# HGRN2 attention and an ELU layer on one core: exponentials of every second group one step ahead, second products with the sums last, decays and loads at other steps

## The chip, the core and the metric

The kernel runs on one core of a Trainium2 chip. The time is that of one execution on the device, in microseconds (us); the figure that counts is the median of several executions. A profile is one execution of its own, recorded by the hardware, and its time is compared with itself only. Engines by their names in the profile: PE multiplies matrices (PEld loads its weights), DVE, ACT and POOL work element by element, SP issues transfers (DMA).

## The reference

Two blocks follow each other. The first is a linear attention with a decaying state, for 4 batches of 8 heads, 768 tokens and 48 numbers per head:

```
f = sigmoid(f_logit)
for t in tokens:
    state = f[t] * state + outer(k[t], v[t])
    y[t]  = q[t] @ state
```

The second takes y as 3072 tokens of 384 numbers and computes `elu(x @ w_in) @ w_out` with 2048 hidden numbers, where elu(h) is h above zero and exp(h) - 1 below. Inputs and result are float32 in meaning; the weights arrive as float64 and are cut to float32 in the first part of the kernel.

## The kernel before

**Units.** The 3072 tokens are cut in 12 units of 256. Every unit goes through attention (PE: `transposed`, `advance`, `scores`, `outputs`, `carried`), gives a tile `xt` of sixteen 128x128 blocks, and this tile goes through the layer. The layer of units 0 and 1 is done plainly, in half steps T = 0 to 31 (`up` and `down`). Units 2 to 11 are done by a scheme with fewer products: `blend` (L937) first makes 12 sums of pairs of xt's blocks in six instructions, numbered 0 to 5 here after their place in `X_SUMS`; number 4 writes blocks 8 and 15. Then a unit has four **groups**. A group (`n`, 40 in all) is 256 of the hidden numbers, 20 products of 128x128x128 in five **phases** (`PHASES`, L428; `phase`, L953), written to two PSUM banks. The first product of a unit's first phase reads block 8.

**From a phase to the second product.** ACT copies parts of a bank to a tile `vals` (L967), DVE adds copies and banks to each other (`joins`, L945: `JOIN3` and `MID` after phase 3, `JOIN4` and `LAST` after phase 4). `LAST` completes the hidden numbers h. `exp_quad` (L1269) then gives ACT two pairs of Relu and Exp for the group (L975, L976), and one step later `elu` (L992) lets DVE take the maximum (L995) and POOL make four sums for each of the two halves of the group (L1005), eight POOL instructions. `down` (L1009) multiplies with `w_out` in seven products of 128x128x192 per half, `todo` (L1041). Three of the seven use the elu's result as it is, four use the sums `s`, which POOL makes in the order s[0], s[2], s[1], s[3]. A unit's last half is followed by an evacuation: ACT copies a bank (L1065) and DVE adds up (L1064).

**The order of the work.** All is written out by hand, and each engine runs its instructions in the order of the program. From T = 32 on the loop at L1278 counts **steps** s = 0 to 99, two half steps each (T = 32 + 2s). A step issues, in this order: the plan of the even half step; two phases, with joins; `MID` and `LAST`; the elu's due (L1293); the plan of the odd half step; a fixed number of second products (`CHUNKS`, L1267: 7, 7, 7, 7, 0, 6, 6, 6, 5, 5); the exponentials due (L1298). Ten steps make a unit, with four groups in them. A group with an even number has its `LAST` in the first phase of step 2 or 7 of the ten, one with an odd number in the second phase of step 4 or 9.

**The plan** (`at_step`) places everything else. For a unit u whose base step is t: `load` (L465, eight DMAs on SP), `gates` (L662, two ACT instructions), three `decays` and one `settle` (`D3`, `D4`), `transposed`, `both`, `outputs` and `carried` (`A3`), and `blend` (`BL`). One `decays(p)` (L695) is a scan (L681) and a reciprocal (L686) on DVE, two scalings on POOL (L676; one for p = 0), and for p = 2 two DMAs on SP (`move`, L688). `settle` (L710) is a small DVE instruction and three scalings on POOL. Before the scheme starts, `w_sums` (L576) combines blocks of `w_in` and `combine` (L918) parts of `w_out`, on DVE and POOL.

Of the kernel before, what the change touches and what calls it, by code (L numbers as in the profile page):

```python
# [356 lines left out]
def fast(ctx: ExitStack, tc: tile.TileContext, q, k, v, f_logit, w_in, w_out, out, flag, outer):  # L357
# [18 lines left out]
    nc = tc.nc  # L376
# [29 lines left out]
    A1 = (2, 8, 10, 11)  # L406
    D2 = (16, 18, 20, 22)
    A2 = (23, 25, 25, 26, 27, 28)
    D3 = (-7, -5, -3, -1)
    D4 = (-9, -6, -4, -1)  # L410
    A3 = (3, 9, 12, 13)
    BL = 16
    BL2 = 29
# [13 lines left out]
    EARLY = 10  # L427
# [11 lines left out]
    MID = (ALU.add, (1, 5), (1, 5), None, (9, 11)), (ALU.subtract, (8, 9), (5, 5), None, (8, 12))  # L439
    JOIN4 = (ALU.add, (3, 6), (2, 11), 0, (0, 2)), (ALU.subtract, 2, 3, 0, 3)  # L440
    LAST = ((ALU.add, (3, 7), (3, 10), None, (4, 7)),)
    PLACES = ((6, ((1, 0), (0, 0), (1, 1), (0, 1))), (0, ((0, 1), (1, 1), (1, 0), (0, 0))))
    USUAL = ((0, 0), (0, 1), (1, 0), (1, 1))

    FULL = (slice(0, 64), slice(64, 128))
# [123 lines left out]
    def w_block(q, n):  # L569
        if n >= 12:  # L570
            return extra[:, q, n - 12]
        i, k = divmod(n, NKT)
        i = (0, 2, 3, 1)[i]
        return wis[:, q, i // 2, k, i % 2]

    def w_sums(e, q, some):  # L576
        for to, a, b, sign in W_SUMS[some]:
            e.tensor_tensor(
                out=w_block(q, to), in0=w_block(q, a), in1=w_block(q, b), op=ALU.add if sign > 0 else ALU.subtract
            )  # L580
# [81 lines left out]
    def gates(u, pieces=(NKT,), bias=1):  # L662

        p = 0
        for n in pieces:
            a = qkf[u % NB]["f"][:, p : p + n, 0]
            nc.scalar.activation(a, a, AF.Exp, scale=-1.0)
            if bias:
                nc.scalar.activation(a, a, AF.Copy, bias=1.0)
            p += n  # L670
# [216 lines left out]
    def at_step(step, *todo):  # L887
        plan.setdefault(step, []).extend(todo)
# [48 lines left out]
    def blend(u, e, some):  # L937

        x = xts[u]
        for to, a, b in X_SUMS[some]:  # L940
            e.tensor_tensor(out=pick(x, to), in0=pick(x, a), in1=pick(x, b), op=ALU.subtract)  # L941
# [67 lines left out]
    def down(P):  # L1009
        m, j = order[P]  # L1010
        if j == 0:
            pms[m] = [ps.tile([128, DM], FP32, tag=f"m{i + (m < DIRECT)}", name=f"psM{m}_{i}") for i in range(NW if m < DIRECT else 4)]
        pm, (g, where) = pms[m], gs.pop(P)
        ends = dict(start=(j == 0), stop=(j == NP - 1))
        if m < DIRECT:
            for i in range(2):
                for t in range(NW):
                    nc.tensor.matmul(  # L1018
                        pm[t][:], lhsT=g[:, 2 * i + t], rhs=wo[:, 2 * j + i, :],
                        start=(j == 0 and i == 0), stop=(j == NP - 1 and i == 1),  # L1020
                    )
            if j == NP - 1:
                o = (outer if (NU - m) % 2 else sb).tile([128, 2, DM], FP32, tag="o", name=f"o{m}", bufs=1)
                for t in range(NW):
                    nc.scalar.copy(o[:, t], pm[t][:])
                    t0 = m * U + t * 128
                    nc.sync.dma_start(out=out[t0 : t0 + 128, :], in_=o[:, t])
                del pms[m]
            return
        a = [[g[:, where.index((i, t))] for i in range(2)] for t in range(2)]  # L1030
        b = [[wo[:, 2 * j + i, h * DH : (h + 1) * DH] for h in range(2)] for i in range(2)]
        plain = PLAIN if m == DIRECT else 0
        if j < plain:

            alone = ((3, 0), (2, 0)), ((2, 1), (3, 1))
            todo = [(*alone[t][h], a[t][i], b[i][h]) for i in range(2) for t in range(2) for h in range(2)]
            starts = ((3, 0), (2, 0)) if j == 0 else ()
        else:
            s = ss.pop(P)
            c = [combos[i][:, j] for i in range(4)]  # L1040
            todo = [  # L1041
                (0, 0, a[0][0], b[0][0]), (3, 0, a[0][1], b[1][0]), (0, 1, s[:, 1], c[1]),
                (1, 0, s[:, 0], c[0]), (1, 1, s[:, 2], c[2]), (2, 1, a[1][1], c[3]), (2, 0, s[:, 3], b[1][1]),
            ]
            if j == plain:
                todo = todo[3:] + todo[:3]
            starts = ((0, 0), (3, 0), (1, 0), (2, 1)) if j == 0 else ((0, 0), (1, 0)) if j == plain else ()
        started = set()
        for n, (bank, half, x, y) in enumerate(todo):
            first = (bank, half) in starts and bank not in started  # L1050
            started.add(bank)
            if n:
                yield
            nc.tensor.matmul(  # L1054
                pm[bank][:, half * DH : (half + 1) * DH], lhsT=x, rhs=y,
                start=first, stop=(j == NP - 1), skip_group_check=True,
            )
        if j == NP - 1:
            p = [[pm[i][:, h * DH : (h + 1) * DH] for h in range(2)] for i in range(4)]
            o = (outer if (NU - m) % 2 else sb).tile([128, 2, DM], FP32, tag="o", name=f"o{m}", bufs=1)  # L1060
            u2 = sb.tile([128, DH], FP32, tag="u2", name=f"u2_{m}", bufs=1)
            u43 = sb.tile([128, 2, DH], FP32, tag="u43", name=f"u43_{m}", bufs=1)
            flat = o[:].rearrange("p t f -> p (t f)")
            add = lambda to, x, y: nc.vector.tensor_tensor(out=to, in0=x, in1=y, op=ALU.add)  # L1064
            (nc.vector.tensor_copy if m == NU - 1 else nc.scalar.copy)(u2[:], p[0][0])  # L1065
            add(flat[:, 0:DH], p[3][0], u2[:])
            add(u2[:], p[0][1], u2[:])
            add(u43[:], pm[1][:].rearrange("p (h f) -> p h f", h=2), u2[:].unsqueeze(1).broadcast_to([128, 2, DH]))
            add(flat[:, 3 * DH :], p[1][0], u43[:, 1])
            if plain:  # L1070
                add(flat[:, 3 * DH :], p[3][1], flat[:, 3 * DH :])
            add(flat[:, DH : 3 * DH], pm[2][:], u43[:].rearrange("p h f -> p (h f)"))
            def store(*queues):
                for t in range(2):
                    for h in ((1, 0) if t else (0, 1)):
                        queues[t].dma_start(
                            out=out[m * U + t * 128 : m * U + (t + 1) * 128, h * DH : (h + 1) * DH],
                            in_=o[:, t, h * DH : (h + 1) * DH],
                        )

            if m == NU - 1:
                left.append(store)
            else:
                store(nc.sync, nc.sync)
            del pms[m]
# [70 lines left out]
    a = qkf[1]["f"][:, 0:NKT, 0]  # L1156
# [38 lines left out]
    for n in range(1, NFT):  # L1195
        t = min(max(needs[n][0] - 2, 0), n) + 2 * (n == NFT - 1)
# [17 lines left out]
        at_step(12 + n, lambda n=n: w_sums(nc.gpsimd, slice(0, 2), slice(n, n + 1)))  # L1214
        at_step(22 + n, lambda n=n: w_sums(nc.gpsimd, slice(2, 4), slice(n, n + 1)))
    for n in range(EARLY, len(W_SUMS)):
        at_step(26 + (n - EARLY) // 2, lambda n=n: w_sums(nc.vector, slice(0, 2), slice(n, n + 1)))
        at_step(32 + n - EARLY, lambda n=n: w_sums(nc.gpsimd, slice(2, 4), slice(n, n + 1)))
    at_step(BL2, lambda: blend(2, nc.vector, slice(0, 3)), lambda: blend(2, nc.gpsimd, slice(3, 6)))
    base = lambda u: u * NFT if u < PLAIN_UP else PLAIN_UP * NFT + (u - PLAIN_UP) * 20  # L1220
    for u in range(3, NU):
        t = base(u - 1)
        for n in range(6):
            at_step(t + BL + n // 2, lambda u=u, n=n: blend(u, nc.gpsimd, slice(n, n + 1)))
        at_step(base(u - 2), lambda u=u: load(u))
        at_step(t - (8 if u == 3 else 10), lambda u=u: gates(u))
        attention(u, [t + i for i in (D3 if u == 3 else D4)], [t + i for i in A3])
    for n in range(NR):
        t = base(3) + (base(NU - 1) - base(3)) * n // NR + RR
        at_step(t, lambda n=n: reread(n))  # L1230
# [30 lines left out]
    exps, elus = {}, {}  # L1261

    def take(n):
        for _ in range(n):
            next(stream, None)
# [3 lines left out]
    def exp_quad(n, s):  # L1269
        for i in range(2):  # L1270
            frm, where = PLACES[i]
            P = PLAIN_UP * NP + 2 * n + i
# [5 lines left out]
    for s in range(5 * total // 2):  # L1278
        T = PLAIN_UP * NFT + 2 * s
        for f in plan.pop(T, ()):  # L1280
            f()
        done = []
        for i in (2 * s, 2 * s + 1):
            n, i = divmod(i, 5)
            phase(n, i)
            if i > 2:
                joins(n, JOIN3 if i == 3 else JOIN4)
                done.append((n, MID if i == 3 else LAST))
        for n, todo in done:
            joins(n, todo)  # L1290
            if todo is LAST:
                exps[s + 1] = n
        for P in elus.pop(s, ()):  # L1293
            elu(P)
        for f in plan.pop(T + 1, ()):
            f()
        take((4, 4, 3, 3)[s] if s < 4 else CHUNKS[s % 10])
        if s in exps:  # L1298
            exp_quad(exps.pop(s), s)
# [55 lines left out]
```

## Time and profile before

| what | value |
|---|---|
| median of 3 runs | 587.03 us (585.92 to 589.24) |
| the profiled execution's own time | 588.51 us |
| its span, first to last instruction | 586.7 us |
| busy: PE, DVE, ACT, POOL | 547.3, 391.9, 315.9, 316.8 us |
| granted PE clock, mean | 0.992 |
| one unit in the scheme (second products of step 35 to those of step 45) | 280.27 to 325.24 us |

The time splits into a start with plain units (to about 120 us), nine units with attention beside them, of 45 us each, a last unit without attention, and a tail of second products. In the answers of the trace a line has the start and the length in us, engine, line of the code, operation, output and input tiles, shapes, and in brackets the idle time of the engine before it and what ended that. PE shows two instructions for each float32 product.

### The profile page before, as it was taken

To read this page: it belongs to the slowest core of one execution; us is meant where nothing else is said; L and a number is where in the kernel's file an instruction comes from. 1 tells how busy PE (TensorE), PEld (TensorE's weight loads), DVE (VectorE), ACT (ScalarE), POOL (GpSimd) and SP (SyncE) were. 2 spreads that over 40 slices of the span, in tenths; PEclk is the share of its full clock that TensorE was granted. 3 is DMA by queue.
4 is the path that set the end of the run, shared out by engine and by line. 5 is a ranking of instruction groups with operands and counts; after the bars stand their busy time and mean duration, and the time that the engine had idled before them with its cause. 6 is when DMAs were issued, how large, how long until landed. Compare 5 with 4: busy or idle time off the path is not lost.

```text
span 586.7 us, 15572 instructions
## 1 busy us (share of the span) xinstructions
PE 547.3 (93%) x6294; PEld 495.4 (84%) x6294; DVE 391.9 (67%) x720; ACT 315.9 (54%) x643; POOL 316.8 (54%) x556
## 2 busy tenths in 40 slices
PE   6799999988999999999999999999999999999876
PEld 3477678877989989889889889889889889899775
DVE  8888884977855945845955955864873973643641
ACT  3387853325455664665656656556656646544440
POOL 6600366695673672682682583484484385264343
PEclk9999999989999999999999999999999999999998
DMA  8999880050061081071071161152152121110001
GB/s 206 259 245 232 235 198 10 8 129 29 8 183 56 8 208 54 11 208 34 32 199 37 38 169 52 53 142 75 54 130 88 51 75 29 56 35 1 28 2 32
DMA packets 39473, 54.28 MB, mean 93 GB/s; under 512 B 4032, under 2 KB 29216, under 8 KB 39392
## 3 DMA queue, kind: packets, MB, share of 16 engines
q1 hardware_dynamic: 38592, 52.61, 34.2%
q8 instruction: 51, 0.84, 0.6%
q10 hardware_dynamic: 800, 0.59, 0.5%
q14 instruction: 30, 0.25, 0.1%
HBM read 45.02 MB, written 4.72 MB: 85 GB/s over the span
## 4 chain that ended last, share of the span: by engine, by line
PE 57%; DVE 27%; POOL 5%; issue 5%; ACT 3%; DMA 2%; ACTq 0%; DVEq 0%; POOLq 0%
PE psM L1054 25%; PE psH L961 19%; DVE vals L951 13%; PE psH L985 5%; DVE gg L995 4%; POOL sums L1005 4%; DVE f L686 3%; PE psM L1018 2%; PE psY L802 2%; DVE o L1064 2%; ACT area L630 1%; DVE u L1064 1%; DVE f L681 1%; PE psT L724 1%; DMA f<-f 1%
## 5 line engine op out<-in xcount | busy, mean ns | idle before, releaser
L1005 POOL TENSOR_TENSOR sums<-gg 128x128 f32<-128x128 f32 x172 | 93.0, 560 | 189.3 <-DVE gg L995 178.4
L967 ACT COPY vals<-psH 128x512 f32<-128x512 f32 (+1 forms) x120 | 64.1, 550 | 169.9 <-PE psH L961 100.5
L961 PE MATMUL psH<-xt,wi 128*128 128x128 f32 x880 | 139.1, 277 | 4.2 <-DVE gg L995 2.3
L961 PE MATMUL psH<-xt,area 128*128 128x128 f32 x720 | 126.0, 279 | 2.5 <-DVE vals L951 1.4
L951 DVE TENSOR_TENSOR vals<-vals,psH 128x256 f32<-128x256 f32 (+1 forms) x160 | 61.4, 384 | 98.0 <-PE psH L961 51.3
L961 PEld LDWEIGHTS psH<-xt,wi 128*128 128x128 f32 x880 | 118.7, 193 | 7.0 <-issue 3.5
L1054 PE MATMUL psM<-area,sums 128*128 128x192 f32 x516 | 107.8, 338 | 15.6 <-POOL sums L1005 15.6
L961 PEld LDWEIGHTS psH<-xt,area 128*128 128x128 f32 x720 | 104.2, 192 | 6.6 <-POOL xt L941 3.7
L1054 PEld LDWEIGHTS psM<-area,sums 128*128 128x128 f32 x516 | 84.1, 191 | 23.9 <-POOL sums L1005 21.9
L1054 PE MATMUL psM<-wo,gg 128*128 128x192 f32 x376 | 77.2, 330 | 1.9 <-DVE gg L995 1.6
L1054 PEld LDWEIGHTS psM<-wo,gg 128*128 128x128 f32 x376 | 62.1, 192 | 4.0 <-DVE gg L995 3.8
L686 DVE RECIPROCAL f<-f 128x256 f32<-128x256 f32 x36 | 62.8, 1748 | 1.1
L976 ACT ACTIVATE gg<-gg 128x512 f32<-128x512 f32 x96 | 60.5, 630 | 3.1
L951 DVE TENSOR_TENSOR vals<-vals 128x256 f32<-128x256 f32 x120 | 56.4, 483 | 2.1
L676 POOL TENSOR_TENSOR k<-k,f 128x256 f32<-128x256 f32 x48 | 39.0, 815 | 29.2 <-DVE f L681 19.0
L995 DVE SCALAR_TENSOR_TENSOR gg<-gg,vals 128x512 f32<-128x512 f32 x80 | 51.6, 685 | 0.8 <-ACT gg L976 0.5
L975 ACT ACTIVATE gg<-vals 128x512 f32<-128x512 f32 x80 | 49.6, 620 | 3.2 <-DVE vals L951 3.2
L985 PE MATMUL psH<-xt,wi 128*128 128x256 f32 x192 | 45.1, 384 | 2.3 <-DVE xt L883 1.7
L676 POOL TENSOR_TENSOR q<-q,f 128x256 f32<-128x256 f32 x48 | 37.0, 771 | 18.8 <-DMA f<-f 15.7
L1064 DVE TENSOR_TENSOR o<-psM,u 128x192 f32<-128x192 f32 (+1 forms) x33 | 13.1, 421 | 50.4 <-ACT u L1065 50.0
L1005 POOL TENSOR_TENSOR sums<-gg,sums 128x128 f32<-128x128 f32 x86 | 43.0, 500 | 6.7
L1054 PE MATMUL psM<-wo,sums 128*128 128x192 f32 x172 | 43.4, 334 | 0.4
(110 smaller groups left out, 771.2 us busy)
## 6 DMA issues: line engine op xcount, KB each, us to landing
area<-in_moe_w_out_dram SPq DMA_DIRECT2D x8, 768.0 KB, 10.8
again<-in_moe_w_in_dram SPq DMA_DIRECT2D x16, 384.0 KB, 4.9
again<-in_moe_w_out_dram SPq DMA_DIRECT2D x16, 384.0 KB, 3.8
k<-in_k_dram SPq DMA_DIRECT2D x12, 384.0 KB, 4.4
q<-in_q_dram SPq DMA_DIRECT2D x12, 384.0 KB, 5.5
v<-in_v_dram SPq DMA_DIRECT2D x12, 384.0 KB, 5.9
area<-in_moe_w_in_dram SPq DMA_DIRECT2D x8, 576.0 KB, 9.2
out_dram<-o SPq DMA_DIRECT2D x42, 96.0 KB, 1.7
```

The costliest lines, as they stand in the source:

```text
L676: e.tensor_tensor(out=t[n][:, p], in0=t[n][:, p], in1=t["f"][:, p, "kq".index(n)], op=ALU.mult)
L686: nc.vector.reciprocal(f[:, p, 1], f[:, p, 0])
L951: nc.vector.tensor_tensor(out=pick(v, to), in0=x, in1=y, op=op)
L961: nc.tensor.matmul(bank[:, slot], lhsT=w_block(q, w), rhs=xts[m][:, x], start=(i < 2 and t == 0), stop=True, skip_group_check=True,)
L967: nc.scalar.copy(v[:, at : at + size], bank[:, frm : frm + size])
L975: nc.scalar.activation(g[:], h, AF.Relu, scale=-1.0)
L976: nc.scalar.activation(g[:], g[:], AF.Exp, scale=-1.0)
L985: nc.tensor.matmul(ph[:, i], lhsT=wi[j][:, kt, i * 128 : (i + 1) * 128], rhs=xts[m][:, 2 * kt : 2 * kt + 2].rearrange("n t f -> n (t f)"), ...
L995: nc.vector.scalar_tensor_tensor(out=g[:], in0=g[:], scalar=-1.0, in1=phs.pop(P), op0=ALU.add, op1=ALU.max)
L1005: nc.gpsimd.tensor_tensor(out=s[:, i], in0=x, in1=y, op=op)
L1054: nc.tensor.matmul(pm[bank][:, half * DH : (half + 1) * DH], lhsT=x, rhs=y, start=first, stop=(j == NP - 1), skip_group_check=True,)
L1064: add = lambda to, x, y: nc.vector.tensor_tensor(out=to, in0=x, in1=y, op=ALU.add)
```

## The change

- `D3` of (-7, -5, -3, -1) becomes (-9, -6, -3, 1); `D4` of (-9, -6, -4, -1) becomes (-17, -15, -5, 1) and is for unit 4 alone; later units have `D5` = (-19, -15, -5, 1). The numbers are half steps, counted from t.
- Exponentials of groups with an even number are issued at the end of the step of their `LAST`, not of the next; their elu's follow one step earlier too.
- In `exp_quad` the two halves of a group change places, and `w_block` changes the blocks of `w_in` accordingly.
- In `down` the product (2, 1), which needs no sum, moves from the sixth place to the third; the product (0, 1), which needs s[1], from the third to the sixth.
- `blend`: two of six instructions in each of the half steps 16, 17, 18 become four in 16 and two in 18.
- `load` and `gates` move: load by 0 half steps for unit 3, 3 for unit 4, 6 for the others ahead; gates from 8 or 10 half steps ahead of t to 11, 19 and 21.
- Nine `w_sums` on DVE start at T = 23, not 26.

No instruction is added or left out.

```diff
-    D3 = (-7, -5, -3, -1)
-    D4 = (-9, -6, -4, -1)
+    D3 = (-9, -6, -3, 1)
+    D4 = (-17, -15, -5, 1)
+    D5 = (-19, -15, -5, 1)
...
-    PLACES = ((6, ((1, 0), (0, 0), (1, 1), (0, 1))), (0, ((0, 1), (1, 1), (1, 0), (0, 0))))
+    PLACES = ((0, ((0, 1), (1, 1), (1, 0), (0, 0))), (6, ((1, 0), (0, 0), (1, 1), (0, 1))))
...
-        i = (0, 2, 3, 1)[i]
+        i = (2, 0, 1, 3)[i]
...
-                (0, 0, a[0][0], b[0][0]), (3, 0, a[0][1], b[1][0]), (0, 1, s[:, 1], c[1]),
-                (1, 0, s[:, 0], c[0]), (1, 1, s[:, 2], c[2]), (2, 1, a[1][1], c[3]), (2, 0, s[:, 3], b[1][1]),
+                (0, 0, a[0][0], b[0][0]), (3, 0, a[0][1], b[1][0]), (2, 1, a[1][1], c[3]),
+                (1, 0, s[:, 0], c[0]), (1, 1, s[:, 2], c[2]), (0, 1, s[:, 1], c[1]), (2, 0, s[:, 3], b[1][1]),
             ]
             if j == plain:
-                todo = todo[3:] + todo[:3]
+                todo = todo[2:5] + todo[:2] + todo[5:]
...
-        at_step(26 + (n - EARLY) // 2, lambda n=n: w_sums(nc.vector, slice(0, 2), slice(n, n + 1)))
+        at_step(23 + (n - EARLY) // 2, lambda n=n: w_sums(nc.vector, slice(0, 2), slice(n, n + 1)))
...
-            at_step(t + BL + n // 2, lambda u=u, n=n: blend(u, nc.gpsimd, slice(n, n + 1)))
-        at_step(base(u - 2), lambda u=u: load(u))
-        at_step(t - (8 if u == 3 else 10), lambda u=u: gates(u))
-        attention(u, [t + i for i in (D3 if u == 3 else D4)], [t + i for i in A3])
+            at_step(t + BL + n // 4 * 2, lambda u=u, n=n: blend(u, nc.gpsimd, slice(n, n + 1)))
+        at_step(base(u - 2) - (0, 3, 6)[min(u - 3, 2)], lambda u=u: load(u))
+        at_step(t - (11, 19, 21)[min(u - 3, 2)], lambda u=u: gates(u))
+        attention(u, [t + i for i in (D3, D4, D5)[min(u - 3, 2)]], [t + i for i in A3])
...
             if todo is LAST:
-                exps[s + 1] = n
+                exps[s + n % 2] = n
```

## The prediction

> **What bounds the kernel now.** I read the busy times first, then PE's waits, then the timelines of one unit.
>
> ```profile
> span 586.7 us, 15572 instructions
> PE 547.3 (93%) x6294; PEld 495.4 (84%) x6294; DVE 391.9 (67%) x720; ACT 315.9 (54%) x643; POOL 316.8 (54%) x556
> ...
> PE psM L1054 <- POOL sums L1005: 15.6, 21, 1.4
> ```
>
> PE is busy for 93% of the span, so only its waits can go, 39 us in all, a part of them at the start. The largest is that second products wait for POOL's sums, 21 times. PE through one unit, step 35 to 45:
>
> ```profile
> 280.27 1.01 PE L1054 MATMUL psM<-area,sums 128*128 128x192 f32 x4 [0.51 <-POOL sums L1005]
> ...
> 282.81 1.16 PE L802 MATMUL psY<-at,v 64*64 64x64 f32 x64
> ...
> 292.88 0.68 PE L961 MATMUL psH<-xt,wi 128*128 128x128 f32 x4 [0.18 <-DVE vals L951]
> ...
> 296.81 0.38 PE L961 MATMUL psH<-xt,area 128*128 128x128 f32 x2
> ...
> 299.67 0.49 PE L1054 MATMUL psM<-wo,sums 128*128 128x192 f32 x2
> 300.25 0.94 PE L961 MATMUL psH<-xt,area 128*128 128x128 f32 x6
> ...
> 302.34 0.92 PE L1054 MATMUL psM<-wo,gg 128*128 128x192 f32 x4
> 304.08 1.24 PE L1054 MATMUL psM<-area,sums 128*128 128x192 f32 x6 [0.82 <-POOL sums L1005]
> ...
> 305.81 0.38 PE L961 MATMUL psH<-xt,area 128*128 128x128 f32 x2
> ...
> 308.47 0.82 PE L1054 MATMUL psM<-wo,gg 128*128 128x192 f32 x4
> ...
> 310.75 0.38 PE L961 MATMUL psH<-xt,area 128*128 128x128 f32 x2
> ...
> 322.84 0.94 PE L961 MATMUL psH<-xt,area 128*128 128x128 f32 x6
> ```
>
> Seven second products without a wait take 308.47 to 310.75, 2.28 us, so 0.326 each. Step 35's six take 280.27 to 282.81, 2.54 instead of 1.96, and began 0.51 late: 1.1 us lost to sums. Step 40's seven take 302.34 to 305.81, 3.47 instead of 2.28: 1.2 us. Step 38's phase, at 292.88, comes 0.2 late: the joins that free its bank stood behind a reciprocal on DVE. That is some 2.5 us of a unit's 45.
>
> **The change part by part.** *Exponentials, elu's and sums of even groups a step earlier.* The same instructions. The sums that step 35 and step 40 wait for are then begun a step, some 4.5 us, sooner: both losses go. What the earlier instructions are put ahead of must be counted. On ACT four exponentials, 2.5 us, now come before a phase's copy:
>
> ```profile
> 294.27 0.59 ACT L967 COPY vals<-psH 128x512 f32<-128x512 f32 x1 [1.78 <-PE psH L961]
> ...
> 295.87 0.63 ACT L975 ACTIVATE gg<-vals 128x512 f32<-128x512 f32 x1
> ```
>
> They began at 295.87 and will begin a step earlier, near 291.4, so they end near 294, and the copy need not move. At nothing: the phase that needs the copy comes at 296.81, 1.9 us behind its end, which is the cover; beyond it PE would be held microsecond by microsecond. On POOL it isn't so:
>
> ```profile
> 289.02 1.57 POOL L1005 TENSOR_TENSOR sums<-gg 128x128 f32<-128x128 f32 x2 [4.58 <-DVE gg L995]
> ...
> 293.47 1.11 POOL L676 TENSOR_TENSOR k<-k,f 128x256 f32<-128x256 f32 x1
> ...
> 295.22 1.42 POOL L941 TENSOR_TENSOR xt<-xt 128x256 f32<-128x256 f32 x2
> 296.59 0.74 POOL L676 TENSOR_TENSOR k<-k,f 128x256 f32<-128x256 f32 x1
> ...
> 297.96 3.10 POOL L941 TENSOR_TENSOR xt<-xt 128x256 f32<-128x256 f32 x4
> 302.43 1.18 POOL L1005 TENSOR_TENSOR sums<-gg 128x128 f32<-128x128 f32 x2 [1.36 <-PE psH L961]
> ...
> 306.30 0.73 POOL L676 TENSOR_TENSOR q<-q,f 128x256 f32<-128x256 f32 x1
> ```
>
> From 289.02 to the last blend POOL never rests: eight sums (step 36's group), k and q, two blends, k and q, four blends. Blend 4 is the third of these four, so it ends near 300.2, and PE's first phase of the next unit, which reads its block 8, starts at 300.25, though the product before it was issued at 299.67 and PE was free at 300.0. Blend 4 thus is on the path already. After the change the program's order on POOL is: eight sums of step 36, k and q of `decays(2)` (odd half of step 37), blends 0 to 3 (step 38, even half), **the eight sums of group 2 of the unit (step 38's elu's), and only then blends 4 and 5 (step 39)**. One k-and-q pair is gone from the front (now far earlier), eight sums are new.
>
> When does blend 4 end? Eight sums: 4.45 (289.02 to 293.47) beside DVE's scan, 3.87 (302.43 to 306.30) without. A pair k, q: 1.75 (293.47 to 295.22) or 1.37 (296.59 to 297.96). Four blends: 2.74 (twice 295.22 to 296.59) or 3.10. One: 0.7 or 0.78. The start, 289.02, is set by PE's phase 3 through joins and elu of an odd group, which don't move. Low: 289.02 + 3.87 + 1.37 + 2.74 + 3.87 + 0.7 = 301.6. High: 289.02 + 4.45 + 1.75 + 3.10 + 4.45 + 0.78 = 303.55. I take 302.2, nearer to low, as the scan and reciprocal that ran beside the first sums move to later. PE then waits from about 299.8 to 302.2, 2.4 us, and from there to the end of step 40's products needs 2.09 - 0.2 (a short wait at 302.34) + 2.28 = 4.2: 306.4 instead of 305.8. The blend takes back 0.6 more than step 38's and step 40's waits gave. With step 35's 1.1, less 0.1 (below), a unit comes out 0.4 us shorter (bounds: 1.0 shorter to 0.95 longer). Eight units with attention: **-3.2 us** (-8 to +7.6).
>
> *The clock.* A wait of 2.4 us has a second price. Stretches of 3.41 us; the columns are length, busy time of PE, PEld, DVE, ACT and POOL, granted clock, share and GB/s of the DMA:
>
> ```profile
> 119.97:123.38 3.41, 1.20 (x8) 0.74 (x6) 3.41 (x6) 0.48 (x1) 3.41 (x6) 1.00 0.54 90
> 123.38:126.79 3.41, 2.95 (x13) 2.95 (x14) 3.12 (x4) 0.41 (x1) 3.33 (x5) 0.50 0.74 215
> 143.86:147.28 3.42, 2.18 (x13) 1.58 (x12) 3.35 (x8) 2.05 (x5) 2.65 (x6) 1.00 0.02 5
> 567.13:570.54 3.41, 0.92 (x4) 0.62 (x4) 2.63 (x6) 2.41 (x4) 2.15 (x3) 1.00 0.00 0
> 570.54:573.95 3.41, 3.40 (x11) 3.40 (x12) 0.51 (x1) 0.00 (x0) 3.29 (x8) 0.50 0.02 7
> ```
>
> And the gap in the first of them, on PE:
>
> ```profile
> 123.84 1.22 PE L961 MATMUL psH<-xt,wi 128*128 128x128 f32 x4 [2.31 <-DVE gg L995]
> ```
>
> After a stretch with 1.20 or 0.92 us of PE work the next ran at half clock, which cost half of its busy 2.95 and 3.40, 1.6 us; after one with 2.18 it didn't. The limit lies in between. If stretches start anywhere, a wait of 2.4 us lies whole in one in 1.0 of 3.41 cases, or is cut in two; its larger part reaches 2.2 us (1.20 left) in 40% of cases and 1.23 us (2.18 left) in 97%. Eight boundaries: 3 to 8 drops. I take four, nearer to the row of 1.20 since a whole wait leaves 1.0: **+6.4 us** (0 to +12.8). In the Trainium skill, "TensorE: Matmul & The Clock Gate", section "Why this matters for your kernels", only idle gaps over some 3 us are to be avoided. By that rule no boundary drops and the sum is 6.4 lower; the drop at 123.38, behind a gap of 2.31, speaks against it.
>
> *Order in `down`.* Three products ahead of the first sum instead of two: 0.33 us more cover. (0, 1) comes three places, 0.98 us, later, and the evacuation waits for it:
>
> ```profile
> 317.89 0.32 ACT L1065 COPY u<-psM 128x192 f32<-128x192 f32 x1 [0.39 <-PE psM L1054]
> ...
> 321.40 0.29 DVE L951 TENSOR_TENSOR vals<-psH,vals 128x128 f32<-128x128 f32 x1
> ```
>
> `JOIN3`, which follows it on DVE, ends at 321.7, so 322.7 after; its bank's next writer is the phase at 322.84. Attention's products cover it, just; `JOIN4` I charge 0.1. In the last unit, without attention, the cover is missing:
>
> ```profile
> 545.82 0.91 PE L961 MATMUL psH<-xt,area 128*128 128x128 f32 x6 [1.12 <-DVE vals L951]
> ...
> 549.22 1.01 PE L1054 MATMUL psM<-area,sums 128*128 128x192 f32 x4 [1.20 <-POOL sums L1005]
> ```
>
> The wait of 1.12 grows by 0.98, and the wait for sums, 1.20 and the 0.6 inside the six products as in step 35, goes: -0.8.
>
> *Decays, gates, loads, `w_block`, halves.* Same instructions. `decays` now stand behind `JOIN4` and `LAST` of steps 32 and 37 and in step 30, where DVE has little else; the elu's behind step 32's come some 2 us before the evacuation. `settle` is needed by `scores` four steps later. On SP eight loads now stand ahead of the move of f:
>
> ```profile
> 288.44 1.22 SPq L838 DMA_DIRECT2D xt<-xt  x2
> ...
> f<-in_f_logit_dram SPq DMA_DIRECT2D x12, 288.0 KB, 4.2
> ```
>
> They follow the transfer of xt, issued by 289.7, so f lands near 294; the gates on ACT come in step 39, from 297 on. The move, issued near 296, is needed at 303. All at nothing; if f came late, ACT's copies and PE would be held by as much.
>
> *Before the scheme and its first unit.* `w_sums` and a decay fill time in which DVE was idle, so the wait of 2.31 us at step 0 and its drop (1.5) go. But unit 4's first decay, the reciprocal's 1.75 and a scan, now stands ahead of `JOIN4` in step 2, which PE's phase in step 3 waits for, and the elu's ahead of the evacuation in step 3:
>
> ```profile
> L686 DVE RECIPROCAL f<-f 128x256 f32<-128x256 f32 x36 | 62.8, 1748 | 1.1
> ```
>
> The gain is near 4. So is the loss, as PE comes sooner and `JOIN4` later: 0 (-4, if the gain stays, to +3, if that wait drops the clock too and f is late).
>
> *Tail.* Group 38's sums are early, so the last 28 products run through:
>
> ```profile
> 568.26 0.92 PE L1054 MATMUL psM<-wo,gg 128*128 128x192 f32 x4 [1.65 <-DVE gg L995]
> 570.55 2.29 PE L1054 MATMUL psM<-area,sums 128*128 128x192 f32 x6 [1.38 <-POOL sums L1005]
> ...
> 580.43 0.49 PE L1054 MATMUL psM<-wo,sums 128*128 128x192 f32 x2
> ```
>
> From 566.6 (568.26 less 1.65), 28 x 0.326 = 9.1, to 575.7 instead of 580.43 + 0.33 = 580.8; the last evacuation starts 0.98 later against that: -4.1.
>
> Sum: -3.2 + 6.4 + 0 - 0.8 - 4.1 = **-1.7 us**. The profiled execution took 588.51 (span 586.7 and 1.8 around it), 1.48 over the median 587.03: 586.8 for it and 585.3 for the median.
>
> **The rivals.** (1) *The clock holds*: at most two drops. For it: the limit may lie under the 1.0 to 1.2 us left, and the cut waits; against it the row at 123.38. -8.1 + 0 to 3.2: 579 to 582. The Trainium skill's rule above would give this time. (2) *Slower: blends 4 and 5 behind the sums* let the clock fall at every unit's start. For it: POOL's unbroken row from 289.02. It decides from seven drops on (-8.1 + 11.2 = +3.1), or from an end of blend 4 at 303 (+0.8 for each unit) with six. Eight drops and 303: -8.1 + 12.8 + 6.4 = +11; so 590 to 598. (3) *The blends don't hold PE*: phase 0 starts at 300.0. Then a unit gains 0.25 there and the 2.5 of its waits less 0.1: 2.65, eight times 21, with 4.9 elsewhere: 561. Against it the order of POOL's program. (4) A load or the gates late: each microsecond at nine units, 590 and more.
>
> **How the numbers follow.** Forecast 0.38 (own range 582 to 589), rival 1 0.27, rival 2 0.24, rival 3 0.06, rival 4 0.05. A measurement can tell 0.5%, 2.9 us, from no change: below 584.1 is faster, over 590 slower. Forecast: 0.12 faster, 0.23 same, 0.03 slower; rival 1 and 3 faster, 0.33; rival 2: 0.21 slower, 0.03 same; rival 4: 0.04 slower, 0.01 same. Together 0.45, 0.27, 0.28. The range 575 to 595 leaves out rival 3 and the far end of rival 2.
>
> **What would show it.** Right: PE's first product of a unit's phase 0 waits some 2.4 us for POOL xt L941; the wait for sums L1005 in step 5 and step 0 is gone; half clock in some stretches behind units' starts; the last 28 products in one row. Wrong: no wait for xt (rival 3); PE's mean granted clock unchanged (rival 1); ACT waiting for f (rival 4).

## The result and the profile after

The changed kernel is slower: 609.35 us (median of 4, 608.61 to 612.11) against 588.13 us (median of 4, 585.92 to 590.55) of the kernel before, run beside it. The ratio is 1.037, with a 95% interval of 1.031 to 1.042. The forecast was 585.3, the range 575 to 595. The profiled execution took 609.11 us, with a span of 607.4 (before 588.51 and 586.7), and its mean granted clock is 0.965 (before 0.992). Behind L414 the lines of the code have numbers one higher than before. Medians leave out one execution of a kernel below, the one with four filler matmuls, that took 957.43 us at a mean granted clock of 0.558.

From the page of the kernel after, span and busy times:

```profile
span 607.4 us, 15590 instructions
...
PE 550.8 (91%) x6294; PEld 509.8 (84%) x6294; DVE 401.2 (66%) x720; ACT 314.9 (52%) x643; POOL 331.2 (55%) x556
```

The same instructions keep PE busy 3.5 us longer and POOL 14.4 us longer. PE's waits of the kernel after (engine, tile and line that waits, what it waits for, us in all, times, longest):

```profile
PE psH L962 <- POOL xt L942: 35.3, 9, 4.2
PE psH L962 <- DVE vals L952: 5.8, 3, 3.4
```

The 21 waits for POOL's sums, 15.6 us before, are gone. In their place stands a wait that was not there: 35.3 us for the blends' tile `xt`, at the starts of nine units (steps 10 to 90). PE at one of them, step 40, in the timeline of the kernel after:

```profile
308.10 0.49 PE L1055 MATMUL psM<-wo,sums 128*128 128x192 f32 x2
312.83 1.65 PE L962 MATMUL psH<-xt,area 128*128 128x128 f32 x6 [4.24 <-POOL xt L942]
...
318.16 0.49 PE L1055 MATMUL psM<-wo,sums 128*128 128x192 f32 x2
```

PE is free at 308.6 and stands for 4.24 us. Before, the last product ended at 300.16 by its line in the prediction, and the same phase came 0.09 us behind it. Of the nine waits seven are 4.24 or 4.25 us, step 80's is 3.79, and step 90's, ahead of the unit without attention, 1.79. POOL ahead of it, in the timeline of the kernel after:

```profile
297.87 1.19 POOL L1006 TENSOR_TENSOR sums<-gg 128x128 f32<-128x128 f32 x2 [11.41 <-DVE gg L996]
...
302.31 0.73 POOL L677 TENSOR_TENSOR k<-k,f 128x256 f32<-128x256 f32 x1
303.00 1.19 POOL L677 TENSOR_TENSOR q<-q,f 128x256 f32<-128x256 f32 x1
304.14 3.48 POOL L942 TENSOR_TENSOR xt<-xt 128x256 f32<-128x256 f32 x4
307.59 0.86 POOL L1006 TENSOR_TENSOR sums<-gg 128x128 f32<-128x128 f32 x2
...
312.05 1.53 POOL L942 TENSOR_TENSOR xt<-xt 128x256 f32<-128x256 f32 x2
```

This is the order that the prediction wrote down: eight sums, k and q, four blends, eight sums, and only then blend 4, the first of the last two. It takes from 297.87 to 312.78, 14.9 us without a pause, and phase 0 begins 0.05 later.

Where the time went can be read from four places. PE's phase 0 of steps 10 and 80 and the phase of step 95, before and after, from the timelines:

```profile
165.43 0.94 PE L961 MATMUL psH<-xt,area 128*128 128x128 f32 x6
...
480.18 0.94 PE L961 MATMUL psH<-xt,area 128*128 128x128 f32 x6
```

```profile
168.44 0.97 PE L962 MATMUL psH<-xt,area 128*128 128x128 f32 x6 [4.24 <-POOL xt L942]
...
506.34 0.95 PE L962 MATMUL psH<-xt,area 128*128 128x128 f32 x6 [3.79 <-POOL xt L942]
...
572.74 0.91 PE L962 MATMUL psH<-xt,area 128*128 128x128 f32 x6 [2.03 <-DVE vals L952]
```

| stretch | before | after | difference |
|---|---|---|---|
| start to step 10 (its wait of 4.24 included) | 165.43 | 168.44 | +3.0 |
| seven units, step 10 to step 80 | 314.75 | 337.90 | +23.2 (3.3 each) |
| step 80 to step 95 (545.82 before) | 65.64 | 66.40 | +0.8 |
| step 95 to the end | 40.88 | 34.66 | -6.2 |

Together +20.7, the difference of the spans. The end gains what was forecast; the loss stands in the units.

The clock falls to half (a granted clock of 0.50) at the starts in steps 10 to 80, eight in all; step 90 keeps it. Stretches of 3.41 us of the kernel after (length; busy time of PE, PEld, DVE, ACT, POOL; granted clock; share and GB/s of the DMA):

```profile
309.16:312.57 3.41, 0.00 (x0) 0.00 (x0) 3.38 (x5) 0.00 (x0) 3.32 (x6) 1.00 0.45 170
312.57:315.98 3.41, 3.15 (x15) 3.15 (x15) 0.12 (x1) 0.48 (x1) 3.33 (x6) 0.50 0.00 0
404.73:408.14 3.41, 1.43 (x9) 1.13 (x7) 3.20 (x9) 0.00 (x0) 3.33 (x7) 1.00 0.96 299
408.14:411.56 3.42, 1.16 (x10) 1.16 (x11) 2.08 (x2) 0.18 (x1) 3.26 (x6) 1.00 0.01 4
411.56:414.97 3.41, 3.41 (x16) 3.41 (x15) 0.00 (x0) 1.99 (x6) 2.33 (x4) 0.50 0.02 5
```

A stretch without work (309.16) and one with 1.16 us (408.14) are followed by half clock, one with 1.43 (404.73) isn't.

### The profile page after: what moved, and what is told of

Its sections match the earlier page's. It is cut to its first block, busy times and chain, and to the rows that moved or that the text cites. A ratio compares the mean times of both kernels' runs of the same rounds, so it can differ in the third digit from the quotient of the medians.

```text
span 607.4 us, 15590 instructions
## 1 busy us (share of the span) xinstructions
PE 550.8 (91%) x6294; PEld 509.8 (84%) x6294; DVE 401.2 (66%) x720; ACT 314.9 (52%) x643; POOL 331.2 (55%) x556
## 4 chain that ended last, share of the span: by engine, by line
PE 76%; POOL 10%; DMA 6%; DVE 4%; issue 1%; ACT 1%; SPq 1%; ACTq 0%; DVEq 0%; POOLq 0%
PE psM L1055 30%; PE psH L962 30%; POOL sums L1006 7%; DMA area<-in_moe_w_in_dram 5%; PE psH L986 5%; PE psM L1019 3%; POOL xt L942 3%; PE psY L803 2%; PE psY L827 2%; PE psU_a L788 2%; PE psS L765 2%; DVE vals L952 2%; PE psT L725 1%; DVE o L1065 1%; DMA f<-in_f_logit_dram 1%
## 5 line engine op out<-in xcount | busy, mean ns | idle before, releaser
L1006 POOL TENSOR_TENSOR sums<-gg 128x128 f32<-128x128 f32 x172 | 100.1, 601 | 201.3 <-DVE gg L996 177.7
L962 PE MATMUL psH<-xt,area 128*128 128x128 f32 x720 | 132.6, 291 | 37.7 <-POOL xt L942 35.3
L962 PE MATMUL psH<-xt,wi 128*128 128x128 f32 x880 | 144.9, 285 | 3.7 <-DVE vals L952 3.4
L962 PEld LDWEIGHTS psH<-xt,area 128*128 128x128 f32 x720 | 110.5, 203 | 42.0 <-POOL xt L942 37.9
L962 PEld LDWEIGHTS psH<-xt,wi 128*128 128x128 f32 x880 | 124.4, 200 | 5.1 <-issue 3.7
L1055 PE MATMUL psM<-area,sums 128*128 128x192 f32 x516 | 104.6, 329 | 0.0
L996 DVE SCALAR_TENSOR_TENSOR gg<-gg,vals 128x512 f32<-128x512 f32 x80 | 64.4, 840 | 10.1 <-ACT gg L977 10.1
L677 POOL TENSOR_TENSOR q<-q,f 128x256 f32<-128x256 f32 x48 | 43.8, 913 | 18.5 <-DMA area<-in_moe_w_in_dram 14.6
L677 POOL TENSOR_TENSOR k<-k,f 128x256 f32<-128x256 f32 x48 | 35.8, 748 | 23.9 <-DVE f L682 15.8
L942 POOL TENSOR_TENSOR xt<-xt 128x256 f32<-128x256 f32 x57 | 46.0, 814 | 4.0 <-DVE xt L942 1.8
L1006 POOL TENSOR_TENSOR sums<-gg,sums 128x128 f32<-128x128 f32 x86 | 42.3, 492 | 6.7
L986 PEld LDWEIGHTS psH<-xt,wi 128*128 128x128 f32 x192 | 35.6, 190 | 8.9 <-DVE xt L884 1.8
```

The costliest lines, as they stand in the source:

```text
L677: e.tensor_tensor(out=t[n][:, p], in0=t[n][:, p], in1=t["f"][:, p, "kq".index(n)], op=ALU.mult)
L962: nc.tensor.matmul(bank[:, slot], lhsT=w_block(q, w), rhs=xts[m][:, x], start=(i < 2 and t == 0), stop=True, skip_group_check=True,)
L986: nc.tensor.matmul(ph[:, i], lhsT=wi[j][:, kt, i * 128 : (i + 1) * 128], rhs=xts[m][:, 2 * kt : 2 * kt + 2].rearrange("n t f -> n (t f)"), ...
L996: nc.vector.scalar_tensor_tensor(out=g[:], in0=g[:], scalar=-1.0, in1=phs.pop(P), op0=ALU.add, op1=ALU.max)
L1006: nc.gpsimd.tensor_tensor(out=s[:, i], in0=x, in1=y, op=op)
L1055: nc.tensor.matmul(pm[bank][:, half * DH : (half + 1) * DH], lhsT=x, rhs=y, start=first, stop=(j == NP - 1), skip_group_check=True,)
```

## The experiments

**The theory.** The blends that stand behind the sums on POOL make PE wait, and the wait makes the clock fall; the rest of the change is harmless or good. **The rivals.** The decays, gates and loads at their new steps cost the time, or the early exponentials do in themselves, and the blends are only the place where it shows; or the clock falls for another reason than the wait.

### All six blends ahead of the sums

```diff
-            at_step(t + BL + n // 4 * 2, lambda u=u, n=n: blend(u, nc.gpsimd, slice(n, n + 1)))
+            at_step(t + BL, lambda u=u, n=n: blend(u, nc.gpsimd, slice(n, n + 1)))
```

> The kernel after, with all six blends at the start of step 8, ahead of that step's eight sums, and nothing else changed. Theory (the wait is blends 4 and 5 behind the sums, and the lost clock follows from that wait): the eight waits of 4.24 us of phase 0 for POOL xt go down to under 0.5, and no unit's start is followed by half clock. 609.4 - 8 x 4.2 - 8 x 1.6 = 563; the sums of step 8's group now end 1.5 us later and may hold the last products of step 10 by up to 1.5, 12 us in all: 560 to 576, faster than before. Rival (decays, loads or the exponentials themselves cost the time, the blends are only where it shows): PE waits somewhere else by as much, and the time stays over 595.

Measured: 560.28 us, ratio 0.954 (0.949 to 0.958). PE's list of waits has no `xt` any more. Busy times on its page, and phase 0 of two neighbouring units in its timeline:

```profile
PE 535.8 (96%) x6294; PEld 496.2 (89%) x6294; DVE 405.2 (72%) x720; ACT 314.9 (56%) x643; POOL 332.4 (59%) x556
```

```profile
269.15 0.91 PE L962 MATMUL psH<-xt,area 128*128 128x128 f32 x6
...
311.16 0.94 PE L962 MATMUL psH<-xt,area 128*128 128x128 f32 x6
```

A unit mostly takes 42.0 us (42.3 in the mean of seven), where it took 45.0 before and mostly 48.0 after (48.3 in the mean). The waits of 35.3 us and 15.0 us of PE's busy time went; the 1.5 us by which the sums end later held nothing. Where two blends stand in POOL's row is worth 49 us. The first two rivals fall: exponentials, decays, gates and loads are all as in the kernel after.

### Work for PE during the wait

```diff
+        if s and s % 10 == 0 and s < 90:
+            warm(4, "a0")
         done = []
         for i in (2 * s, 2 * s + 1):
```

> The kernel after, with four matmuls on the identity (128 columns into 512, into a bank that is free there; their result isn't used) just ahead of phase 0 of the units' starts in steps 10 to 80, so that PE works through most of the wait for POOL xt. The wait itself stays: phase 0 begins as late as before. Theory (half clock follows from PE's idle time): no half clock at the eight starts, 609.4 - 8 x 1.6 = 597, 594 to 600. Rival (the clock falls there for another reason, or the drops were hidden by other waits): half clock stays, or the time stays at 607 to 611.

Measured: 595.97 us, ratio 1.016 (1.011 to 1.020). And with three matmuls instead of four:

> The kernel after, with three matmuls on the identity instead of four ahead of phase 0 of steps 10 to 80 (their result isn't used). PE is then idle for about 4.2 - 3 x 0.87 = 1.6 us at a unit's start. Theory (a stretch of 3.41 us is followed by half clock where PE worked 1.39 us or less in it, so only a gap over 2.0 us can do it): no half clock at the eight starts, mean granted clock 0.99, 609.4 - 8 x 1.6 = 596, as with four. Rival (half clock there has another cause than the idle time): drops remain, 602 to 610.

Measured: 595.6 us, ratio 1.012 (1.007 to 1.017). PE at step 40 of the kernel with three, and the stretches there:

```profile
306.39 2.74 PE L1115 MATMUL psW<-ident 128*128 128x512 f32 x6
310.80 0.94 PE L963 MATMUL psH<-xt,area 128*128 128x128 f32 x6 [1.67 <-POOL xt L943]
```

```profile
308.34:311.76 3.42, 1.75 (x10) 0.96 (x9) 2.29 (x2) 0.00 (x0) 3.26 (x6) 1.00 0.35 134
311.76:315.17 3.41, 3.41 (x26) 3.41 (x26) 0.00 (x0) 2.70 (x8) 2.53 (x4) 1.00 0.00 0
```

Phase 0 still begins 4.4 us behind the last product (306.39 to 310.80), but the clock holds at the eight starts. The late start is left, half clock is gone, and with it 609.35 - 595.97 = 13.4 us with four matmuls and 13.8 with three, 1.7 for each start: half clock follows from PE's idle time and has nearly the price of the prediction, 1.6.

### The exponentials alone, and everything but them

The kernel before with `exps[s + 1] = n` made `exps[s + n % 2] = n`, and the kernel after with the opposite edit.

> The kernel before, with one line of the change alone: the exponentials of even groups a step earlier. Blends 2 to 5 then stand behind the sums of step 8 (in the kernel after only 4 and 5). Theory: phase 0 waits for POOL xt longer than in the kernel after, by about two more blends, 1.5 us: 5 to 6 us at eight starts, with half clock behind each; 612 to 625. Rival (the early exponentials are harmless, and what costs time is the rest): 580 to 590.

> The kernel after, with the exponentials of even groups put back to where they were; order of the products, decays, gates, loads and blends stay as after. Theory: the sums of the even group stand behind all six blends again; no wait of phase 0 for POOL xt over 0.7 us, no half clock at the units' starts, 580 to 592. Rival (decays, gates and loads in their new places cost the time): over 597.

Measured: the exponentials alone 618.87 us, ratio 1.053 (1.049 to 1.058); everything but them 581.36 us, ratio 0.989 (0.985 to 0.994). Two of PE's waits of the former, which has two blends more behind the sums, and its phase 0 at one start:

```profile
PE psH L961 <- POOL xt L941: 33.8, 9, 4.9
PE psH L961 <- ACT psH L969: 6.7, 8, 0.9
```

```profile
319.19 1.59 PE L961 MATMUL psH<-xt,area 128*128 128x128 f32 x6 [3.90 <-POOL xt L941]
```

Both times lie in the expected ranges, and half clock follows at all eight starts, but the wait for `xt` is 4.93 at the first start only; at the other seven it is 3.8 to 3.9, less than 4.24, because PE comes to phase 0 later there by a new wait of 0.9 for ACT. Together they are 4.8, half a microsecond more than 4.24 and not 1.5, and not by the blends: blends 0 to 3 and the sums stand ahead of blend 4 in either order. POOL's row is longer here, 16.1 us, by a second pair k, q, which the kernel after has earlier. So the expectation had the direction right, but not the cause. Without the exponentials the list has no wait for `xt`. So one line of the change makes the loss, and nearly all of it by what it puts ahead of blend 4 on POOL: with all blends in front of the sums the same line takes the time from 581.4 to 560.3.

### The pair k, q away from the blends

```diff
-    D4 = (-17, -15, -5, 1)
-    D5 = (-19, -15, -5, 1)
+    D4 = (-17, -15, -11, 1)
+    D5 = (-19, -15, -11, 1)
```

> The kernel after, with the third decay of units 4 and later, and with it the pair k, q on POOL that stood ahead of blends 0 to 3 in step 8, moved to step 4. This takes 1.9 us from POOL's row ahead of blend 4, so that phase 0 waits about as long as the prediction had it (2.4 us); in the kernel after it was 4.24. Theory (POOL's row sets the wait term by term): blend 4 ends 1.5 to 1.9 us earlier, the wait is 2.3 to 2.8 us, and with it 8 x 1.6 = 13 us go: 609.4 - 13 = 596 if all eight starts still lose clock, 592 to 590 if, as predicted for such a wait, only four or five do. Rival (something other than POOL's row holds the blend, the elu or xt): the wait stays over 3.5 us and the time over 603.

Measured: 579.4 us, ratio 0.986 (0.981 to 0.991), below the least that I expected. PE's wait in all, step 40's phase 0, and the stretches around the starts in steps 10 and 40:

```profile
PE psH L962 <- POOL xt L942: 18.3, 9, 2.2
```

```profile
299.24 1.65 PE L962 MATMUL psH<-xt,area 128*128 128x128 f32 x6 [2.02 <-POOL xt L942]
```

```profile
162.74:166.16 3.42, 1.47 (x10) 1.17 (x8) 3.21 (x9) 0.00 (x0) 3.28 (x6) 1.00 0.65 246
166.16:169.57 3.41, 3.35 (x25) 3.35 (x26) 2.38 (x3) 1.71 (x4) 3.33 (x6) 1.00 0.02 5
295.86:299.28 3.42, 1.40 (x10) 1.10 (x8) 3.21 (x9) 0.00 (x0) 3.26 (x7) 1.00 0.58 229
299.28:302.69 3.41, 3.41 (x16) 3.41 (x17) 2.28 (x2) 0.48 (x1) 3.41 (x5) 0.50 0.00 0
```

The row from the first sum to the end of blend 4 now takes 12.7 us (286.50 to 299.2) instead of 14.9, and the wait is 2.2 us shorter as well: the row sets the wait. Of these 2.2 the pair itself is 1.83; the two sets of sums became 1.0 shorter and the blends 0.6 longer. And of the starts of units only one, step 40, lost its clock. Its stretch held 1.40 us of PE work; one with 1.47 at step 10 kept the clock, like the one with 1.43 above. I had expected four drops or more from waits of 2.3 to 2.8; they were 2.0 (once 2.2), just at the limit, and all but step 40's were cut in two by the border of two stretches. Seven drops and 8 x 2.2 us less, together some 30 us, are the difference of 609.35 and 579.4.

### The order of the products alone, and the rest alone

The kernel before with the new `todo` lists of `down`; and the kernel after with the exponentials and the `todo` lists of before.

> The kernel before with only the order of the products changed as in the kernel after. Before, PE waited 21 times, 15.6 us in all, for POOL sums. Theory (the whole change without the exponentials gained 6.5 us, most of it by this order: three products cover the sums instead of two, and the sums come one by one in between): the waits for sums go down to about 5 us, against 1 us more at step 95: 587.8 - 10.6 + 1 + 1 (the last evacuation) = 579, 578 to 583. Rival (the decays, gates and loads gave the gain, and the order only 0.33 us once or twice a unit): 584 to 588.

> The kernel after, with exponentials and order of the products put back: only decays, gates, loads, blends two steps apart and the swapped halves of the units' first stage are left. The prediction had these at 0 (-4 to +3). From the runs: the whole without exponentials was 6.5 us below before, the order alone 1.9, so if the parts add up, 587 - 4.6 = 582 to 584. Rival (the order's gain needs the decays, and these alone give nothing): 586 to 590. In both the wait of step 0 is gone and one of 3.4 to 4.1 us stands in step 3, with half clock behind it.

Measured: the order 584.82 us, ratio 0.995 (0.990 to 1.001), a miss of the forecast and in the range of the rival; the rest 584.74 us, ratio 0.995 (0.992 to 0.998), between the two expectations. Waits of the kernel with the order alone, and of that with the rest alone:

```profile
PE psM L1054 <- DVE gg L995: 4.4, 11, 1.6
...
PE psM L1054 <- POOL sums L1005: 3.5, 11, 0.3
```

```profile
PE psM L1055 <- POOL sums L1006: 18.9, 21, 1.4
PE psH L962 <- DVE vals L952: 4.6, 2, 3.5
```

The order takes the waits for sums from 15.6 to 3.5 us, but some of it comes back as waits for the elu, and the time shows little of it: a unit takes 44.7 to 45.0 us, where it took 45.0. Moved decays, gates and loads cost nothing in the units, which mostly take 44.4 us with the rest alone. In the first unit step 0's wait of 2.31 is gone and one of 3.5 in step 3 has come. The two parts multiply to 0.990, and together, everything but the exponentials, they gave 0.989: they add up within the noise, though the interval of the order alone includes no gain at all.

### The order with the exponentials early

The kernel with all blends in front, with the `todo` lists of before.

> The kernel with all six blends ahead of the sums (560.3 us), with the products of a group in the order of the kernel before, (0, 1) third instead of sixth. Theory (with the exponentials early, sums are ready anyway, and the new order only makes the evacuation later): step 95's wait of about 2.1 us goes down by 0.98, the last evacuation starts 0.98 earlier, no wait for sums over 0.3 us: 557 to 559. Rival (sums are just in time, the third product's 0.33 us is needed): waits for sums come back, 561 to 566.

Measured: 559.34 us, ratio 0.953 (0.948 to 0.959), with the new order 0.954: no difference. Its waits have this line, which the new order doesn't have:

```profile
PE psM L1055 <- POOL sums L1006: 4.8, 10, 0.8
```

The rival is right that sums are just in time, the theory that step 95 gains (its wait is 1.12, with the new order 2.02); that the two cancel is argued, not shown, as the medians differ by less than the runs of either.

### Unit 4's decays, and the ends of the last two units

On the kernel with all blends in front:

```diff
-    D4 = (-17, -15, -5, 1)
+    D4 = (-15, -11, -5, 1)
```

> The kernel with all six blends ahead of the sums (560.3 us), and unit 4's first two decays moved from steps 1 and 2 to steps 2 and 4, behind those steps' joins. Theory (the scan and reciprocal of unit 4's first decay stand ahead of JOIN4 on DVE, and PE's phase in step 3 waits 3.50 us for it, with half clock behind): wait and drop go, 560.3 - 3.4 - 1.7 = 555, 553 to 557. Rival (the wait moves to the evacuation or to an elu in steps 3 to 5, or the joins are late for another reason): 559 to 562.

Measured: 556.95 us, ratio 0.949 (0.944 to 0.955), within the expectation. The phase of step 3, in the timeline of the kernel with all blends in front and in that of this one:

```profile
133.00 0.68 PE L962 MATMUL psH<-xt,wi 128*128 128x128 f32 x4 [3.50 <-DVE vals L952]
```

```profile
130.55 0.68 PE L962 MATMUL psH<-xt,wi 128*128 128x128 f32 x4 [0.56 <-DVE vals L952]
```

It waits 0.56 us, where it waited 3.50 with the decays in their former place, and no half clock follows. And on top of this:

```diff
+            if j == NP - 1 and m >= NU - 2:
+                todo = [*todo[:2], todo[5], *todo[3:5], todo[2], todo[6]]
```

> The kernel with all six blends ahead of the sums and unit 4's decays moved (557.0 us), with the old order of the products in the last group of the last two units alone, where no attention covers the later evacuation. Theory: step 95's wait of 2.03 us goes down by 0.98, and the last evacuation starts 0.98 earlier: 555.0, 553 to 557. Rival (the evacuation was not what PE waits for there, or the sums are late for the old order): 556 to 559.

Measured: 553.54 us (553.34 to 556.62), ratio 0.943 (0.939 to 0.947). Step 95 of this kernel:

```profile
518.15 0.91 PE L962 MATMUL psH<-xt,area 128*128 128x128 f32 x6 [1.12 <-DVE vals L952]
```

It waits 1.12, as in the kernel before, instead of 2.03. This version beats the kernel before by 34 us and the kernel after by 56.

## Why the prediction was wrong

**What failed is one term: the end of blend 4.** The prediction had POOL's order right and wrote that phase 0 waits for it. It put the row at 302.2 - 289.02 = 13.2 us, "nearer to low, as the scan and reciprocal that ran beside the first sums move to later". It took 14.9, and the count of lost clocks, four, followed the too short wait and came out at eight:

| term | forecast, low to high | measured |
|---|---|---|
| eight sums of step 36 | 3.87 to 4.45 | 4.44 |
| k and q | 1.37 to 1.75 | 1.83 |
| four blends | 2.74 to 3.10 | 3.45 |
| eight sums of step 38 | 3.87 to 4.45 | 4.46 |
| blend 4 | 0.70 to 0.78 | 0.73 |

Every large term is at its upper end or beyond, and the wait was 4.24 instead of 2.4. The reason for taking the low end was false: a scan still ran beside the first sums (at 300.21); additions of `joins` and another scan ran beside the second (from 308.37 and 310.22); and the elu's, which moved a step earlier as well, now ran beside q and the first blend. The prediction had no term for this. DVE and POOL there, in the timeline of the kernel after, instruction by instruction:

```profile
300.21 0.94 DVE L682 TENSOR_TENSOR_SCAN f<-f 128x256 f32<-128x256 f32 x1
...
302.86 0.73 DVE L996 SCALAR_TENSOR_TENSOR gg<-gg,vals 128x512 f32<-128x512 f32 x1
...
303.51 1.22 DVE L996 SCALAR_TENSOR_TENSOR gg<-gg,vals 128x512 f32<-128x512 f32 x1
...
304.14 1.18 POOL L942 TENSOR_TENSOR xt<-xt 128x256 f32<-128x256 f32 x1
...
305.28 0.73 POOL L942 TENSOR_TENSOR xt<-xt 128x256 f32<-128x256 f32 x1
...
308.37 1.60 DVE L952 TENSOR_TENSOR vals<-vals 128x256 f32<-128x256 f32 x3
...
310.22 0.68 DVE L682 TENSOR_TENSOR_SCAN f<-f 128x256 f32<-128x256 f32 x1
```

With q from 303.00 to 304.19 (above) the four alternate: the first elu ends at 303.59, q 0.60 later; the second elu 0.55 behind q; the blend 0.59 behind the elu. But for the first elu, each takes some 0.5 us longer than the same instruction without the other beside it (q 0.73 in the prediction's rows, the next blend 0.73). It is the rule in this trace: of POOL's 128x256 instructions for k, q and blends, the 51 with nothing on DVE beside them took 0.72 to 0.73 us, the 21 with a reciprocal alone (one input) as long, the 25 with an elu alone (two inputs) 1.17 to 1.19. Of what the row took beyond its low bounds, some 2.4 us, q and that blend make 0.9 and the two sets of sums 1.2. Over all elu's, in the groups by line of the kernel before and of the kernel after (busy, mean ns):

```profile
L995 DVE SCALAR_TENSOR_TENSOR gg<-gg,vals 128x512 f32<-128x512 f32 x80 | 51.6, 685 | 0.8 <-ACT gg L976 0.5 <-issue 0.3
```

```profile
L996 DVE SCALAR_TENSOR_TENSOR gg<-gg,vals 128x512 f32<-128x512 f32 x80 | 64.4, 840 | 10.1 <-ACT gg L977 10.1
```

The Trainium skill, "SBUF — State Buffer", section "Who interferes with whom", states it: "A DVE instruction with two SBUF inputs contends with a GpSimd instruction that reads SBUF", and its section "Summary: rules for kernel authors" adds that the second to issue is held until the first is done. The rows agree; they look like one instruction behind the other, not like two at half speed. I hadn't drawn on this in the forecast. That the lengthening comes from lying side by side was read from the rows and not tested by itself. In the kernel with the pair moved away it went to the blends, of which four now take 3.93 us:

```profile
290.56 3.93 POOL L942 TENSOR_TENSOR xt<-xt 128x256 f32<-128x256 f32 x4
```

**The clock.** The price of a drop, 1.6 us, was right to a tenth (1.7 with the fillers). The count was not: eight instead of four, because the wait was longer. The limit, put between 1.20 and 2.18 us of work, lies between 1.40 (half clock followed) and 1.43 (it didn't), so a gap must take at least 2.0 us of one stretch. A wait of 4.24 leaves a piece of 2.12 or more in one stretch wherever it is cut, and 3.41 - 2.12 = 1.29 is below the limit: it drops the clock every time. One of 2.0 does it only where it lies whole in one stretch. With this limit a wait of 2.4 would do it in (1.0 + 2 x 0.4) of 3.41 cases by the prediction's own reckoning, four of eight (an estimate): four was the right count for the wait that it assumed. The Trainium skill's rule, that only gaps over some 3 us matter ("TensorE: Matmul & The Clock Gate", "Why this matters for your kernels"), isn't borne out here: the gap of 2.02 at step 40 above was followed by half clock.

**A unit.** Forecast 0.4 shorter, or 0.4 longer with half a drop; measured 3.3 longer. What the waits for sums and step 38 were worth held: without the wait for `xt` a unit takes 42.0 to 42.3 us, 2.7 to 3.0 below 45.0, where rival 3 had 2.65. On 42.0 to 42.3 come 4.24 and 1.6 to 1.7, which make the 48.0 to 48.3.

**The smaller terms held.** Step 95's wait was to grow from 1.12 by 0.98 and is 2.03. From there to the end the sums' 1.2 and 0.6 and the tail's 4.1 make 5.9; measured 6.2. The parts at nothing cost nothing in the units. The transition, 0 (-4 to +3), hid two terms: the wait of step 0 went, and unit 4's first decay ahead of `JOIN4` made a new one of 3.43, as written, with half clock behind; moving unit 4's first two decays brought 3.3 us. Step 90's wait of 1.79 was in no term: the prediction counted eight units, and nine have blends.

**Rivals 1 to 3 each came true in some kernel; rival 4, a late load or late gates, in none of them.** The kernel after is rival 2, whose 590 to 598 was too low: eight drops were counted, but the end of blend 4 was taken as 303 and was 303.9 on that scale, 0.9 more at eight starts, which is 7 of the 10 us that its +11 lacked. The kernel with the pair moved away is rival 1, 579 to 582, at 579.4, though there the clock holds because the wait is 2.0 and not 2.4. The kernel with the blends in front is rival 3, 561, at 560.3. So mechanisms and prices were right, and the choice among them hung on 1.7 us in a row of 13.

## What to carry to other kernels

When a change puts work ahead of the last writer of a tile that the bounding engine reads, sum that engine's row at the upper ends, and look for what else moved beside it on an engine whose instructions lengthen its own (here DVE and POOL). If the result is that the order decides, move the writer in front first: here two blends four microseconds earlier turn +3.7% into -4.6%. A wait near the clock's limit is a cliff, not a slope: a wait of 2.0 us cost 2.0 at seven starts of eight, one of 4.2 cost 5.9 at every one.

## What the runs showed that was not expected

- The limit of the clock is sharp in the scheme: stretches at full clock with 1.40 us of PE work and less were followed by half clock, 1.43 and 1.47 were not. In the start it is less so: in the kernel with three fillers this stretch, with 1.51 us in 64 instructions, was followed by half clock:

```profile
21.62:25.04 3.42, 1.51 (x64) 1.14 (x64) 2.91 (x5) 0.00 (x0) 1.75 (x3) 1.00 1.08 230
25.04:28.45 3.41, 2.78 (x73) 2.42 (x74) 2.39 (x3) 0.33 (x2) 2.51 (x2) 0.50 1.04 267
```

- An elu on DVE and an instruction for q or the blends on POOL take some 0.5 us longer where one begins while the other runs (840 instead of 685 ns in the mean of the 80 elu's); the inputs of both lie in SBUF.
- Why the order alone takes 12 us of waits for sums away and moves the median by only 1.9 was not followed further.
